# Block-sparse attention with a soft mixture of experts: wider value products for shared key blocks, and a new table of priorities

## The chip, the core and the metric

The kernel runs on one core of a Trainium2 chip. Its engines work side by side, each through its own list of instructions in the order of that list: TensorE (PE; its weight loads are shown apart as PEld), VectorE (DVE), ScalarE (ACT), GpSimd (POOL) and SyncE (SP), whose queue starts most DMA transfers. The metric is the device time of one execution in microseconds (us). Three runs of the kernel before took 310.15, 309.86 and 308.01 us; the median is 309.86.

## The reference

There are 4 batches of 8 heads, 768 positions and 64 dimensions. Positions are cut into 24 blocks of 32. A query block sees the key blocks beside it and itself, the first and the last block, and three sampled blocks; the first and the last query block see everything. What follows is a soft mixture of experts over all 3072 rows.

```python
mask = np.abs(blk_i - blk_j) <= 1
mask = mask | (blk_i == 0) | (blk_j == 0) | (blk_i == n_blocks - 1) | (blk_j == n_blocks - 1)
for qb in range(n_blocks):
    for kb in sampled_blocks[qb]:
        mask[qb * block:(qb + 1) * block, kb * block:(kb + 1) * block] = True
attn = softmax(where(mask, scale * q @ k.T, -1e9))      # softmax written out in the source
x = (attn @ v) as rows of 512                           # 8 heads side by side
logits = x @ phi                                        # 32 slots
slot_input = softmax(logits, axis=0).T @ x              # over all 3072 rows
slot_out = relu(slot_input @ w1[e]) @ w2[e]             # 8 experts, 4 slots each
out = softmax(logits, axis=1) @ slot_out
```

## The kernel before, in words

All data are fp32. One program matmul becomes two MATMUL instructions and two weight loads on the chip (a transpose on TensorE stays one of each).

**Attention.** The 22 inner query blocks of a batch are taken in pairs, called units. A first unit stands alone; the other ten form five tiles of two units, that is of four query blocks. For each query block `stage_k` (lines 450 to 478) copies the key blocks it sees into a staging tile `kst` of 256 columns, as eight places of 32: three neighbours, the first and the last block, three sampled ones. POOL copies the neighbours and first/last blocks, ACT or POOL the sampled ones. In the kernel before the neighbours stand at columns 0 to 95 or 32 to 127 by whether the block's number is odd or even, first and last at 128 to 191, and the sampled blocks in what is left. TensorE then makes the scores `s` (line 542), DVE the row maximum `nm` (557), ACT the exponential `p` (562), and DVE turns `p` by 32x32 blocks into `ptt` (569), so that place number c of the staging tile is row block c of `ptt`.

**Value products.** `av_heads` (642 to 675) multiplies the turned weights by the value blocks `v`, half of the heads at a time (`r` is 0 or 1; in each, `g` is the upper or lower 64 rows of TensorE). The weights are the stationary operand and the value block (130 columns: two heads of 64 and a column of ones) is moved past it. A half of a tile is, in this order: the first and last key block for all four query blocks (128 weight columns, 4 program matmuls); for each unit the two key blocks that both its query blocks see (64 columns, 8 matmuls); the one neighbour left to each query block (32 columns, 8 matmuls); and 24 sampled ones of 32 columns out of `vrs`, to which POOL copies the sampled value blocks (487). Each key block is thus multiplied unit by unit, although three query blocks in a row share it. There are 20 such tiles, so 40 halves, and 4 lone units. `av_mm` (line 634) issues every value product; the two query blocks that see everything (`dense`, 788 to 795) use it too, with 96 products in one go, called `avd`.

**After attention.** DVE divides by the sum of weights to give `x` (629); TensorE transposes it (`mxt`, 830), and four tiles form a group with logits `ml` (873), a transposed copy `lt` (891), transposed weights `md` (914), sums `ms` (923). At the end of attention a chain of small steps joins the groups, and the expert products (`pf`, `pso`) and output products (`po`) follow, with 33.6 MB of weights coming in by DMA and 6.3 MB of output leaving.

**Order.** Every step is a task with a cost, dependencies and a key: its number in the sequence plus an offset by its kind from the table `OFF` (lines 65 to 69). `Plan.run` (107 to 206) walks through them with its own costs and sets the order in which every engine gets its instructions. `ni`, the number of TensorE instructions of a task, enters there. So a new table gives another order on every engine.

Of the kernel before, what the change touches and what calls it, by code (L numbers as in the profile page):

```python
# [20 lines left out]
BLK, NB, NR = 32, 24, 3  # L21
# [9 lines left out]
VPOS = lambda k: (k - 1) % (NB + 1)  # L31
# [30 lines left out]
HEAD = -4096  # L62
SWITCH, FETCH, AHEAD, BLOCK = 0.22, 4.3, 0.5, 256
BACK = {"PE": 0.05, "DVE": -0.07, "ACT": -0.1, "POOL": -0.06, "SP": 0.0, "NONE": 0.0}
OFF = {"acc": 7.76, "av": -0.34, "av1": -0.31, "av2": -0.36, "avo": -1.17, "avo1": 1.4, "ce": -7.77, "cm": -0.63,
       "cn": 4.13, "dav": -0.96, "davo": -2.61, "dexp": 1.91, "do": 2.49, "dqk": -0.74, "dt": 2.51, "dtop": 9.1,
       "dtrn": -6.76, "exp": 1.01, "ldq": -0.52, "lexp": 1.53, "lg": -2.72, "lo": 1.64, "lp": -4.13, "lt": 3.97,
       "ltop": 3.66, "qk": -0.78, "scl": 15.38, "smp": 2.29, "sum": 2.97, "top": -2.96, "trn": -2.23, "vst": -2.29,
       "xt": 4.21, "xto": 3.13}
E_ = mybir.EngineType  # L70
MAN = {E_.PE, E_.DVE, E_.Activation, E_.Pool}
LAG = {"PE": 0.28, "DVE": 0.08, "ACT": 0.06, "POOL": 0.1, "SP": 0.0, "NONE": 0.0}
# [10 lines left out]
class Plan:  # L83
# [6 lines left out]
    def add(self, f, opts, deps, key, acq=(), byte=0, pre=None, pace=False, kind=None, mode=None, ni=0):  # L90
        t = Task(f, opts if isinstance(opts, list) else [opts], deps, key + OFF.get(kind, 0.0), acq, byte, pre, pace,
                 kind, mode, ni)
        self.tasks.append(t)
        return t
# [115 lines left out]
def attn_moe_kernel(ctx, tc, qT, kT, vfull, vtab, sampled, phi, w1, w2, out):  # L210
    nc = tc.nc
    PE, ACT, DVE, POOL, SP = nc.tensor, nc.scalar, nc.vector, nc.gpsimd, nc.sync
# [107 lines left out]
    ktile, vtile = [None] * B, [None] * B  # L320
# [6 lines left out]
    for n in range(NVR):  # L327
        n = (B * (NB - 2) + n) % NVR
        vrs[n] = pst.tile([P, 2, NR, 2 * D1], F32, name=f"vrs{n}")

    nq = [0]
# [54 lines left out]
    add = plan.add  # L386
# [17 lines left out]
    use = []  # L404
# [42 lines left out]

    fresh, nst, nvs = {}, [0], [0]

    def stage_k(b, i, n, use):  # L450
        k = nst[0] % NKST
        nst[0] += 1
        st, new = kst[k], fresh.get(k) != b
        fresh[k] = b

        w, r0 = (0, 96) if i % 2 else (32, 0)

        def fixed(t):
            kv = ktile[b]
            if new:  # L460
                POOL.tensor_copy(out=st[:, :, 128:192].rearrange("p c (g s) -> p c g s", g=2),
                                 in_=kv.rearrange("p c (g s) -> p c g s", g=NB)[:, :, 0:NB:NB - 1, :])
            POOL.tensor_copy(out=st[:, :, w:w + 96], in_=kv[:, :, (i - 1) * BLK:(i + 2) * BLK])  # L463

        def sampled_(t):
            for j, o in enumerate((r0, 192, 224)):
                src = ktile[b][:, :, ds(t.vals[j] * BLK, BLK)]
                if t.eng == "ACT":
                    ACT.activation(out=st[:, :, o:o + BLK], in_=src, func=AF.Copy, scale=1.0)  # L469
                else:  # L470
                    POOL.tensor_copy(out=st[:, :, o:o + BLK], in_=src)  # L471

        f = add(fixed, ("POOL", 0.95 if new else 0.52), [t_k[b]], n - 4, acq=[("kst", use)], kind="fix")
        r = add(sampled_, [("ACT", 0.72), ("POOL", 0.86)], [f, t_sreg], n - 2.5,
                pre=lambda e: block_numbers(sreg, i, e, NB - 1), kind="smp")
        k_use[b].extend([f, r])
        use.extend([f, r])
        return st, r
# [44 lines left out]
    def plan_pair(b, g, n):  # L523
        T = tile_of(b, (g + 1) // 2)
        w = 1 if g and g % 2 == 0 else 0
        u = Rec()
        u.g = g
        kd, ku = [], []
        for r in range(2):
            use = []  # L530
            kd.append(stage_k(b, 2 * g + 1 + r, n, use))
            ku.append(use)
        t_q, q_use = plan_q(u, b, g + 1, n)
        s_use = [[], []]
# [18 lines left out]
        for r in range(2):  # L553
# [21 lines left out]
            for j in range(2):  # L575
                t_e.append(add(lambda t, r=r, j=j, exp=exp: exp(t, r, j), ("ACT", 0.48), [t_m] + t_e, n + 0.2 + 0.01 * r, kind="exp",
                               acq=[("p", p_use)] if j == 0 else []))
            s_use[r].append(t_e[1])
            acq = []
            if w == 0:  # L580
                T.pt_use = getattr(T, "pt_use", {})
                T.pt_use[r] = []
                acq = [("ptt", T.pt_use[r])]
# [4 lines left out]
        for r in range(2):  # L588
            use = []
# [42 lines left out]
    def av_mm(av, o, m, g, r, lhsT, rhs, start, stop):  # L632
        av = av[g][o:o + m] if isinstance(av, list) else av[o:o + m, g]
        PE.matmul(av[:, r * 2 * D1:(r + 1) * 2 * D1].rearrange("p (a d) -> p a d", a=2),  # L634
                  lhsT=lhsT, rhs=rhs, start=start, stop=stop)

    G2 = [(g, slice(64 * g, 64 * g + 64)) for g in range(2)]

    def new_av(T):
        T.av = psA.tile([P, 2, 512], F32, tag="av", name="av", bufs=1)  # L640

    def av_heads(T, rs_):

        vt, us = vtile[T.b], T.units
        one = len(us) == 1
        m = 64 * len(us)
        for n, c in enumerate((4, 5)):
            for r in rs_:
                for g, s_ in G2:
                    av_mm(T.av, 64 * r if one else 0, m, g, r, T.pt[r][s_, c, 0:m // BLK].rearrange("p j q -> p (j q)"),  # L650
                          vt[s_, :, VPOS((0, NB - 1)[n]), r, :], n == 0, False)
        for c in (1, 2):
            for w, u in enumerate(us):
                for r in rs_:
                    for g, s_ in G2:
                        av_mm(T.av, 64 * r if one else 64 * w, 64, g, r,
                              T.pt[r][s_, c, 2 * w:2 * w + 2].rearrange("p j q -> p (j q)"),
                              vt[s_, :, VPOS(2 * u.g + c), r, :], False, False)
        for n in range(NR + 1):
            for w, u in enumerate(us):  # L660
                for r in rs_:
                    for j in range(2):
                        i = 2 * u.g + 1 + j
                        for g, s_ in G2:
                            if n == 0:

                                k, c = (i - 1, 0) if j == 0 else (i + 1, 3)
                                if k in (0, NB - 1):
                                    continue
                                v_ = vt[s_, :, VPOS(k), r, :]  # L670
                            else:
                                c = ((3, 0)[j], 6, 7)[n - 1]
                                v_ = u.vst[j][s_, :, n - 1, r, :]
                            av_mm(T.av, (64 * r if one else 64 * w) + 32 * j, 32, g, r, T.pt[r][s_, c, 2 * w + j], v_,
                                  False, n == NR)

    def plan_av(T, n):
        deps = T.turned + T.staged + [t_v[T.b]]
        use, x_use = [], T.x_use
        if len(T.units) == 1:  # L680
            def both(t):
                new_av(T)
                av_heads(T, range(2))

            def out(t):
                for r in range(2):
                    av_out(T, T.av, 64 * r, 64 * r + 64, slice(r, r + 1), 0)
            t_a = add(both, ("PE", 2.1), deps, n + 0.5, acq=[("av", use)], kind="av1", mode="63", ni=176)
            T.out = [add(out, ("DVE", 1.68), [t_a], n + 0.6, kind="avo1")]
        else:  # L690

            T.split = T is tiles.get((B - 1, NT - 1))

            def heads(t, r):
                if T.split and r == 0:
                    T.av = T.av0 = [psA.tile([P, 512], F32, tag="s", name="av", bufs=SB) for g in range(2)]
                elif r == 0 or T.split:
                    new_av(T)
                av_heads(T, (r,))
            if T.split:  # L700
                t_0 = add(lambda t: heads(t, 0), ("PE", 2.05), deps, n + 0.5, acq=[("s", use)] * 2, kind="av", mode="W3", ni=176)
                last = []
                t_a = add(lambda t: heads(t, 1), ("PE", 2.05), [t_0], n + 0.5, acq=[("av", last)], kind="av", mode="W3", ni=176)
                T.out = [add(lambda t, r=r: av_out(T, T.av if r else T.av0, 0, P, slice(r, r + 1)), ("DVE", 0.8 if r else 1.0),
                             [(t_0, t_a)[r]], n + 0.6, acq=[] if r else [("x", x_use)]) for r in range(2)]
                last.append(T.out[1])
            else:
                t_0 = add(lambda t: heads(t, 0), ("PE", 2.05), deps, n + 0.5, acq=[("av", use)], kind="av", mode="W3", ni=176)
                t_a = add(lambda t: heads(t, 1), ("PE", 2.05), [t_0], n + 0.5, kind="av2", mode="W3", ni=176)
                T.out = [add(lambda t: av_out(T, T.av, 0, P), ("DVE", 1.2), [t_a], n + 0.6, acq=[("x", x_use)], kind="avo")]  # L710
        x_use.extend(T.out)
        use.extend(T.out)
        v_use[T.b].append(t_a)
        T.t_av = t_a
        for u in T.use + list(T.pt_use.values()):
            u.append(t_a)
        if T.t:
            done.append((n, T))
# [346 lines left out]
    for gi in range(6):  # L1065
        Ts = done[4 * gi:4 * gi + 4]
        t_m, k = plan_group(gi, Ts, Ts[-1][0])
# [400 lines left out]
```

## Time and profile before

| | |
|---|---|
| median of 3 runs | 309.86 us |
| profiled execution | 306.71 us, its span 304.9 us, mean granted TensorE clock 0.976 |
| PE busy / in the chain that ended last | 90% / 77% |
| DVE, POOL, ACT busy | 72%, 60%, 54% |
| attention | from about 13 us to about 242 us of the span |

A busy share is a mean over stages. In the profile a MATMUL's time is counted from its start to a modelled end, and many overlap; what one costs is therefore read from the distance between starts, that is from the length of a stretch and the number of matmuls in it, not from its mean duration. "Issue" is idle time for which the profile shows no event that was waited for. The instruction queue of a page's part 3 (q8) is the DMA that brings TensorE's own instructions.

### The profile page before, as it was taken

To read this page: it belongs to the slowest core of one execution; us is meant where nothing else is said; L and a number is where in the kernel's file an instruction comes from. 1 tells how busy PE (TensorE), PEld (TensorE's weight loads), DVE (VectorE), ACT (ScalarE), POOL (GpSimd) and SP (SyncE) were. 2 spreads that over 40 slices of the span, in tenths; PEclk is the share of its full clock that TensorE was granted. 3 is DMA by queue.
4 is the path that set the end of the run, shared out by engine and by line. 5 is a ranking of instruction groups with operands and counts; after the bars stand their busy time and mean duration, and the time that the engine had idled before them with its cause. 6 is when DMAs were issued, how large, how long until landed. Compare 5 with 4: busy or idle time off the path is not lost.

```text
span 304.9 us, 17513 instructions
## 1 busy us (share of the span) xinstructions
PE 273.1 (90%) x7139; PEld 188.7 (62%) x7139; DVE 220.3 (72%) x497; ACT 165.2 (54%) x504; POOL 182.4 (60%) x509
## 2 busy tenths in 40 slices
PE   7599997998999999999989899969987989999950
PEld 7248675775867666777667666847655653355640
DVE  4699967869998689998979899958886545012360
ACT  0877866733966578286687646657633141102450
POOL 2579698696858999593889959329953314000000
PEclk9889999999999999999999999999999899999995
DMA  7936678440375751054666122878889997999998
GB/s 241 402 121 184 183 205 220 132 138 23 93 199 161 196 159 41 6 147 132 185 185 171 45 73 77 206 161 229 218 221 382 406 378 256 399 408 408 359 315 277
DMA packets 31633, 63.61 MB, mean 209 GB/s; under 512 B 5313, under 2 KB 18754, under 8 KB 31554
## 3 DMA queue, kind: packets, MB, share of 16 engines
q1 hardware_dynamic: 31408, 62.37, 64.5%
q8 instruction: 56, 0.92, 1.3%
q14 instruction: 23, 0.19, 0.2%
q10 hardware_dynamic: 146, 0.13, 0.1%
HBM read 56.19 MB, written 6.29 MB: 205 GB/s over the span
## 4 chain that ended last, share of the span: by engine, by line
PE 77%; DVE 6%; issue 5%; DMA 4%; ACT 2%; SPq 1%; POOL 1%; POOLq 1%; DVEq 0%; ACTq 0%
PE av L634 32%; PE s L542 13%; PE avd L634 7%; PE pf L1266 5%; PE pso L1274 4%; PE mxt L830 4%; PE sd L738 3%; DMA out_dram<-ob 2%; PE ml L873 2%; PE ms L923 2%; DMA ktile<-in_kT_dram 2%; DVE ptt L569 1%; DVE cm L1001 1%; PE po L1370 1%; PE pc L1029 1%
## 5 line engine op out<-in xcount | busy, mean ns | idle before, releaser
L487 POOL COPY vrs<-v 128x260 f32 x264 | 95.6, 412 | 24.1 <-PE av L634 16.1
L562 ACT ACTIVATE p<-s,nm 128x256 f32<-128x256 f32 x176 | 72.3, 479 | 23.7 <-DVE nm L557 21.7
L634 PE MATMUL av<-v,ptt 64*64 64x130 f32 (+2 forms) x1728 | 76.0, 288 | 1.6 <-issue 1.3
L634 PEld LDWEIGHTS av<-v,ptt 64*64 64x64 f32 (+2 forms) x1728 | 50.9, 133 | 29.6 <-issue 16.0
L569 DVE STREAM_TRANSPOSE ptt<-p 128x512 f32<-128x512 f32 x88 | 58.7, 692 | 10.1 <-ACT p L562 9.8
L542 PE MATMUL s<-kst,q 64*32 64x256 f32 x1408 | 51.3, 384 | 7.9 <-ACT pd L769 3.5
L557 DVE TENSOR_REDUCE nm<-s 128x2 f32<-128x512 f32 x88 | 55.0, 673 | 3.5 <-PE s L542 3.3
L463 POOL COPY kst<-ktile 128x384 f32<-128x384 f32 x88 | 42.7, 515 | 19.8 <-PE s L542 19.2
L634 PE MATMUL av<-vrs,ptt 64*32 64x130 f32 x2112 | 47.2, 276 | 3.2 <-issue 3.0
L469 ACT ACTIVATE kst<-ktile 128x128 f32 x171 | 38.7, 305 | 11.3 <-PE s L542 10.1
L542 PEld LDWEIGHTS s<-kst,q 64*32 64x32 f32 x1408 | 28.4, 106 | 21.5 <-issue 5.4
L634 PEld LDWEIGHTS av<-vrs,ptt 64*32 64x32 f32 x2112 | 36.2, 106 | 5.8 <-issue 5.3
L769 ACT ACTIVATE pd<-sd,nb 128x384 f32<-128x384 f32 x32 | 16.7, 577 | 18.6 <-DVE nb L764 18.0
L471 POOL COPY kst<-ktile 128x128 f32 x93 | 23.6, 306 | 0.0
L634 PE MATMUL avd<-v,ptd 64*64 64x130 f32 x768 | 22.9, 271 | 0.4 <-DVE x L629 0.3
L634 PEld LDWEIGHTS avd<-v,ptd 64*64 64x64 f32 x768 | 21.7, 132 | 2.1 <-PE s L542 1.6
L380 ACT COPY xT<-mxt 128x512 f32<-128x512 f32 (+1 forms) x22 | 12.1, 567 | 13.0 <-PE mxt L830 12.7
L756 DVE TENSOR_REDUCE nm<-sd 128x1 f32<-128x384 f32 x32 | 16.2, 545 | 2.8 <-PE sd L738 2.8
L629 DVE TENSOR_TENSOR x<-av,rs 128x512 f32<-128x512 f32 (+2 forms) x28 | 16.9, 605 | 1.0
L773 DVE STREAM_TRANSPOSE ptd<-pd 128x384 f32<-128x384 f32 x32 | 16.3, 552 | 1.8 <-ACT pd L769 1.7
L506 POOL TENSOR_SCALAR q<-q 128x256 f32<-128x256 f32 x25 | 10.3, 415 | 11.9 <-DMA q<-in_qT_dram 11.2
L830 PE MATMUL mxt<-ident,x 128*128 128x128 f32 x96 | 14.0, 282 | 3.7 <-issue 1.9
(123 smaller groups left out, 268.5 us busy)
## 6 DMA issues: line engine op xcount, KB each, us to landing
w<-in_w_dram SPq DMA_DIRECT2D x20, 512.0 KB, 8.1
v<-in_w_dram SPq DMA_DIRECT2D x12, 512.0 KB, 10.2
q<-in_qT_dram SPq DMA_DIRECT2D x47, 128.0 KB, 2.9
w<-in_w_dram SPq DMA_DIRECT2D x44, 128.0 KB, 3.3
out_dram<-ob SPq DMA_DIRECT2D x22, 256.0 KB, 3.4
ktile<-in_kT_dram SPq DMA_DIRECT2D x48, 96.0 KB, 2.9
v<-in_w_dram SPq DMA_DIRECT2D x24, 128.0 KB, 4.4
kw<-in_w_dram SPq DMA_DIRECT2D x6, 512.0 KB, 9.1
```

Source lines behind the costliest of these rows:

```text
L463: POOL.tensor_copy(out=st[:, :, w:w + 96], in_=kv[:, :, (i - 1) * BLK:(i + 2) * BLK])
L469: ACT.activation(out=st[:, :, o:o + BLK], in_=src, func=AF.Copy, scale=1.0)
L471: POOL.tensor_copy(out=st[:, :, o:o + BLK], in_=src)
L487: POOL.tensor_copy(out=st[:, :, j:j + 1, :], in_=vf[:, :, ds(t.vals[j], 1), :])
L542: PE.matmul(u.s[r][32 * p:32 * p + 32, j, :], lhsT=u.q[s_, p, j, :], rhs=kd[j][0][s_, p, :], start=True, stop=True)
L557: DVE.tensor_reduce(out=u.nm[r], in_=u.s[r], axis=AX.X, op=ALU.max, negate=True)
L562: ACT.activation(out=u.p[r][:, j, :], in_=u.s[r][:, j, :], func=AF.Exp, bias=u.nm[r][:, j:j + 1], scale=1.0)
L569: DVE.transpose(out=T.pt[r][:, :, 2 * w:2 * w + 2, :].rearrange("p k j q -> p j k q"), in_=u.p[r].rearrange("p j (k q) -> p j k q", k=8))
L629: DVE.tensor_tensor(out=x, in0=a[:, :, :, 0:D], in1=rs[lo:hi].unsqueeze(3).to_broadcast([hi - lo, 2, 2 * n, D]), op=ALU.mult)
L634: PE.matmul(av[:, r * 2 * D1:(r + 1) * 2 * D1].rearrange("p (a d) -> p a d", a=2), lhsT=lhsT, rhs=rhs, start=start, stop=stop)
L769: ACT.activation(out=u.p[r][k], in_=u.s[r][k], func=AF.Exp, bias=u.nb[r], scale=1.0)
L830: PE.transpose(T.px[:, c, :], T.x[:, c * P:(c + 1) * P], ident)
```

## The change

1. `av_heads` calls a new function for the neighbours. It walks through the key blocks that a whole tile sees. A block seen by three query blocks of the tile gets one product of 96 weight columns where these start at row 0 of the tile; where they start at row 32 it is split in one of 32 and one of 64 columns. Per half of a tile this is 2 program matmuls of 96, 6 of 64 and 6 of 32 columns, where there were 8 of 64 and 8 of 32. They come after those of 128 columns, the widest first.
2. So that place c means the same key block for all four query blocks, `stage_k` gets the place `a` (0 to 3) of the query block in its tile: its neighbours stand in places a to a+2, first and last in places 6 and 7, the sampled blocks in the places left free. The copies have the same number and sizes as before.
3. `ni` goes from 176 to 168, and all offsets in `OFF` are new.

```diff
-OFF = {"acc": 7.76, "av": -0.34, "av1": -0.31, "av2": -0.36, "avo": -1.17, "avo1": 1.4, "ce": -7.77, "cm": -0.63,
+OFF = {"acc": 4.35, "av": -0.84, "av1": -0.64, "av2": -1.46, "avo": -2.52, "avo1": 0.46, "ce": 0.57, "cm": -1.57,
...
+    def free_slots(a):
+
+        return [c for c in range(6) if not a <= c < a + 3]
...
-        w, r0 = (0, 96) if i % 2 else (32, 0)
...
-            POOL.tensor_copy(out=st[:, :, w:w + 96], in_=kv[:, :, (i - 1) * BLK:(i + 2) * BLK])
+            POOL.tensor_copy(out=st[:, :, a * BLK:(a + 3) * BLK], in_=kv[:, :, (i - 1) * BLK:(i + 2) * BLK])
...
-            for j, o in enumerate((r0, 192, 224)):
+            for j, o in enumerate(c * BLK for c in free_slots(a)):
...
+    def av_window(T, rs_, width):
+
+        vt, us = vtile[T.b], T.units
+        one, nq = len(us) == 1, 2 * len(us)
+        for c in range(nq + 2):
+            k, lo, hi = 2 * us[0].g + c, max(c - 2, 0), min(c + 1, nq)
+            if k in (0, NB - 1):
+                continue
+            for lo, hi in ((lo, lo + 1), (lo + 1, hi)) if lo and hi - lo == 3 else ((lo, hi),):
+                if hi - lo not in width:
+                    continue
+                for r in rs_:
+                    for g, s_ in G2:
+                        av_mm(T.av, (64 * r if one else 0) + BLK * lo, BLK * (hi - lo), g, r,
+                              T.pt[r][s_, c, lo:hi].rearrange("p j q -> p (j q)"), vt[s_, :, VPOS(k), r, :], False, False)
...
+        for w in (3, 2, 1):
+            av_window(T, rs_, (w,))
+        for n in range(NR):
...
-                t_0 = add(lambda t: heads(t, 0), ("PE", 2.05), deps, n + 0.5, acq=[("av", use)], kind="av", mode="W3", ni=176)
+                t_0 = add(lambda t: heads(t, 0), ("PE", 2.05), deps, n + 0.5, acq=[("av", use)], kind="av", mode="W3", ni=168)
```

How the order on TensorE changes is shown at two places. The first is the beginning of one half of a tile (`av`) in the second batch; the numbers behind a name are buffers, the size is weight columns by moved columns, and xN counts program matmuls. Before:

```order
L634 MATMUL av<-v_69,ptt 128x130 x4
L634 MATMUL av<-v_69,ptt 64x130 x8
L634 MATMUL av<-v_69,ptt 32x130 x8
L634 MATMUL av<-vrs_103,ptt 32x130 x2
L634 MATMUL av<-vrs_104,ptt 32x130 x2
```

With the change:

```order
L636 MATMUL av<-v_69,ptt 128x130 x4
L636 MATMUL av<-v_69,ptt 96x130 x2
L636 MATMUL av<-v_69,ptt 64x130 x6
L636 MATMUL av<-v_69,ptt 32x130 x6
L636 MATMUL av<-vrs_103,ptt 32x130 x2
```

Two of the 64-column and two of the 32-column products have gone, and two of 96 columns are new; the products from `vrs` are as they were.

The second place is TensorE around the dense product (`avd`) of the fourth batch, where steps of the group before (`ms`, `lt`, `mxt`) stand between scores (`s`). Before:

```order
L923 MATMUL ms<-x,d 32x512 x4
L542 MATMUL s<-kst_93,q_99 32x256 x8
L542 MATMUL s<-kst_94,q_99 32x256 x8
L891 MATMUL lt<-ident,lp 128x128
L542 MATMUL s<-kst_95,q_100 32x256 x8
L542 MATMUL s<-kst_96,q_100 32x256 x8
L634 MATMUL avd<-v_69,ptd 64x130 x96
L542 MATMUL s<-kst_93,q_97 32x256 x8
L542 MATMUL s<-kst_94,q_97 32x256 x8
L830 MATMUL mxt<-ident,x 128x128 x8
L634 MATMUL av<-v_69,ptt 128x130 x4
```

With the change:

```order
L927 MATMUL ms<-x,d 32x512 x4
L544 MATMUL s<-kst_93,q_99 32x256 x8
L544 MATMUL s<-kst_94,q_99 32x256 x8
L544 MATMUL s<-kst_95,q_100 32x256 x8
L544 MATMUL s<-kst_96,q_100 32x256 x8
L636 MATMUL avd<-v_69,ptd 64x130 x96
L834 MATMUL mxt<-ident,x 128x128 x8
L544 MATMUL s<-kst_93,q_97 32x256 x8
L544 MATMUL s<-kst_94,q_97 32x256 x8
L636 MATMUL av<-v_69,ptt 128x130 x4
```

`lt` no longer stands between the scores ahead of the dense product, and the transposes `mxt` from behind two score products to directly behind `avd`. Elsewhere the moves are of this kind: steps of a group and transposes pass one half of a tile or one score product; the sequence of tiles is the same.

## Rows read from the trace of the kernel before

**Rows 1.** The page: busy time by engine (part 1) and the chain (part 4).

```profile
PE 273.1 (90%) x7139; PEld 188.7 (62%) x7139; DVE 220.3 (72%) x497; ACT 165.2 (54%) x504; POOL 182.4 (60%) x509
...
PE 77%; DVE 6%; issue 5%; DMA 4%; ACT 2%; SPq 1%; POOL 1%; POOLq 1%; DVEq 0%; ACTq 0%
PE av L634 32%; PE s L542 13%; PE avd L634 7%; PE pf L1266 5%; PE pso L1274 4%; PE mxt L830 4%; PE sd L738 3%; DMA out_dram<-ob 2%; PE ml L873 2%; PE ms L923 2%; DMA ktile<-in_kT_dram 2%; DVE ptt L569 1%; DVE cm L1001 1%; PE po L1370 1%; PE pc L1029 1%
```

**Rows 2.** Window of one stage: length, busy us (instructions) of PE, PEld, DVE, ACT, POOL, clock.

```profile
85.00:135.00 50.00, 48.20 (x1493) 34.05 (x1483) 43.85 (x96) 33.38 (x106) 41.02 (x115) 1.00 0.46 129
```

**Rows 3.** The chain of waits in order of time: start, length, what.

```profile
79.96 5.53 PE avd L634 x192
...
96.38 1.02 PE mxt L830 x8
...
105.67 2.36 PE av L634 x88
```

**Rows 4.** Windows of one half, tile av, PE alone: length, busy (matmuls running).

```profile
105.59:106.24 0.65, 0.64 (x8) 1.00 0.68 196
106.24:106.84 0.60, 0.60 (x18) 1.00 0.80 212
106.84:107.95 1.10, 1.10 (x68) 1.00 0.80 230
```

**Rows 5.** The same view, the first 128-column products one by one.

```profile
105.59:105.81 0.22, 0.21 (x2) 1.00 0.71 223
105.81:105.92 0.11, 0.11 (x4) 1.00 0.89 266
105.92:106.03 0.11, 0.11 (x6) 1.00 0.55 186
```

**Rows 6.** Groups by form on PE: count, busy us, mean ns, idle before.

```profile
L634 PE MATMUL av<-v,ptt 64*128 64x130 f32 x320 | 29.2, 300 | 0.2
```

**Rows 7.** Timeline of PE: start, length, line, shapes, count, idle time before.

```profile
90.28 0.31 PE L634 MATMUL av<-vrs,ptt 64*32 64x130 f32 x4 [0.58 <-issue]
90.40 0.37 PE L542 MATMUL s<-kst,q 64*32 64x256 f32 x1
90.42 0.28 PE L634 MATMUL av<-vrs,ptt 64*32 64x130 f32 x3
90.53 1.09 PE L542 MATMUL s<-kst,q 64*32 64x256 f32 x31
91.55 1.71 PE L634 MATMUL av<-v,ptt 64*128 64x130 f32 x40
93.05 0.95 PE L634 MATMUL av<-vrs,ptt 64*32 64x130 f32 x48
94.30 2.08 PE L542 MATMUL s<-kst,q 64*32 64x256 f32 x64 [0.29 <-issue]
```

**Rows 8.** The page, part 3: the queue that brings TensorE's instructions.

```profile
q8 instruction: 56, 0.92, 1.3%
```

**Rows 9.** Waits of PE: total us, times, longest us.

```profile
PE av L634 <- issue: 4.3, 6, 1.3
...
PE s L542 <- issue: 2.7, 3, 2.3
PE mxt L830 <- issue: 1.9, 1, 1.9
...
PE s L542 <- POOL vrs L487: 1.7, 1, 1.7
PE mxt L830 <- DVE x L629: 1.5, 2, 0.8
```

**Rows 10.** Timeline of PE: the three longest idle times marked issue.

```profile
74.46 0.78 PE L634 MATMUL av<-v,ptt 64*64 64x130 f32 x7 [1.30 <-issue]
...
201.75 1.08 PE L542 MATMUL s<-kst,q 64*32 64x256 f32 x28 [2.28 <-issue]
...
233.96 0.77 PE L830 MATMUL mxt<-ident,x 128*128 128x128 f32 x5 [1.91 <-issue]
```

More of the change, by code (lines that the diff above doesn't have):

```diff
@@ L64 @@
 BACK = {"PE": 0.05, "DVE": -0.07, "ACT": -0.1, "POOL": -0.06, "SP": 0.0, "NONE": 0.0}
-OFF = {"acc": 7.76, "av": -0.34, "av1": -0.31, "av2": -0.36, "avo": -1.17, "avo1": 1.4, "ce": -7.77, "cm": -0.63,
[L66 to L69, printed above, removed]
+OFF = {"acc": 4.35, "av": -0.84, "av1": -0.64, "av2": -1.46, "avo": -2.52, "avo1": 0.46, "ce": 0.57, "cm": -1.57,
+       "cn": 3.06, "dav": 0.22, "davo": 0.82, "dexp": -0.08, "do": 4.06, "dqk": -1.85, "dt": 2.26, "dtop": -0.71,
+       "dtrn": -6.45, "exp": 0.1, "ldq": 6.51, "lexp": 2.4, "lg": 0.27, "lo": 1.31, "lp": -0.77, "lt": 4.58, "ltop":
+       3.52, "qk": -0.87, "scl": 6.6, "smp": 1.49, "sum": 3.39, "top": -0.71, "trn": -2.36, "vst": -2.22, "xt": 3.08,
+       "xto": 3.1}
 E_ = mybir.EngineType
@@ L448, in attn_moe_kernel, with stage_k @@
     fresh, nst, nvs = {}, [0], [0]
-    def stage_k(b, i, n, use):
+    def free_slots(a):
+        return [c for c in range(6) if not a <= c < a + 3]
+    def stage_k(b, i, a, n, use):
         k = nst[0] % NKST
@@ L460, in fixed @@
             if new:
-                POOL.tensor_copy(out=st[:, :, 128:192].rearrange("p c (g s) -> p c g s", g=2),
+                POOL.tensor_copy(out=st[:, :, 192:256].rearrange("p c (g s) -> p c g s", g=2),
                                  in_=kv.rearrange("p c (g s) -> p c g s", g=NB)[:, :, 0:NB:NB - 1, :])
-            POOL.tensor_copy(out=st[:, :, w:w + 96], in_=kv[:, :, (i - 1) * BLK:(i + 2) * BLK])
+            POOL.tensor_copy(out=st[:, :, a * BLK:(a + 3) * BLK], in_=kv[:, :, (i - 1) * BLK:(i + 2) * BLK])
         def sampled_(t):
-            for j, o in enumerate((r0, 192, 224)):
+            for j, o in enumerate(c * BLK for c in free_slots(a)):
                 src = ktile[b][:, :, ds(t.vals[j] * BLK, BLK)]
@@ L530, in plan_pair @@
             use = []
-            kd.append(stage_k(b, 2 * g + 1 + r, n, use))
+            kd.append(stage_k(b, 2 * g + 1 + r, 2 * w + r, n, use))
             ku.append(use)
@@ L646, in av_heads @@
         m = 64 * len(us)
-        for n, c in enumerate((4, 5)):
+        for n, c in enumerate((6, 7)):
             for r in rs_:
@@ L651, in av_heads @@
                           vt[s_, :, VPOS((0, NB - 1)[n]), r, :], n == 0, False)
[L652 to L659, printed above, removed]
+        for w in (3, 2, 1):
+            av_window(T, rs_, (w,))
+        for n in range(NR):
             for w, u in enumerate(us):
@@ L662, in av_heads @@
                     for j in range(2):
-                        i = 2 * u.g + 1 + j
+                        a = 2 * w + j
                         for g, s_ in G2:
[L665 to L675, printed above, removed]
+                            av_mm(T.av, (64 * r if one else 0) + BLK * a, 32, g, r, T.pt[r][s_, free_slots(a)[n], a],
+                                  u.vst[j][s_, :, n, r, :], False, n == NR - 1)
     def plan_av(T, n):
@@ L700, in plan_av @@
             if T.split:
-                t_0 = add(lambda t: heads(t, 0), ("PE", 2.05), deps, n + 0.5, acq=[("s", use)] * 2, kind="av", mode="W3", ni=176)
+                t_0 = add(lambda t: heads(t, 0), ("PE", 2.05), deps, n + 0.5, acq=[("s", use)] * 2, kind="av", mode="W3", ni=168)
                 last = []
-                t_a = add(lambda t: heads(t, 1), ("PE", 2.05), [t_0], n + 0.5, acq=[("av", last)], kind="av", mode="W3", ni=176)
+                t_a = add(lambda t: heads(t, 1), ("PE", 2.05), [t_0], n + 0.5, acq=[("av", last)], kind="av", mode="W3", ni=168)
                 T.out = [add(lambda t, r=r: av_out(T, T.av if r else T.av0, 0, P, slice(r, r + 1)), ("DVE", 0.8 if r else 1.0),
@@ L707, in plan_av @@
             else:
-                t_0 = add(lambda t: heads(t, 0), ("PE", 2.05), deps, n + 0.5, acq=[("av", use)], kind="av", mode="W3", ni=176)
-                t_a = add(lambda t: heads(t, 1), ("PE", 2.05), [t_0], n + 0.5, kind="av2", mode="W3", ni=176)
+                t_0 = add(lambda t: heads(t, 0), ("PE", 2.05), deps, n + 0.5, acq=[("av", use)], kind="av", mode="W3", ni=168)
+                t_a = add(lambda t: heads(t, 1), ("PE", 2.05), [t_0], n + 0.5, kind="av2", mode="W3", ni=168)
                 T.out = [add(lambda t: av_out(T, T.av, 0, P), ("DVE", 1.2), [t_a], n + 0.6, acq=[("x", x_use)], kind="avo")]
```

## The prediction, made before the changed kernel ran

> **What bounds the kernel now.** I read the page first. TensorE is busy 90% of the span and holds 77% of the chain that ended last, 32% in the value products of one line and 7% in the dense ones [rows 1]. The reader is to see that whatever a value product costs on TensorE stands in the time nearly in full, while POOL and ACT, which copy the keys, are not in the chain. In the stage from 85 to 135 us TensorE is busy 48.2 of 50.0 us at the full granted clock of 1.00 (2.4 GHz), and DVE 43.9 us [rows 2]: DVE is the next one behind it.
>
> Then I took one half of a tile apart. In the chain it lasts 2.36 us [rows 3]. Windows show three stretches: 0.65 us for 8 MATMULs of 128 weight columns, 0.60 us for 16 of 64, 1.10 us for 64 of 32 [rows 4]; of the counts there, 2 and 4 still run on from the stretch before. Inside the first stretch two MATMULs start in each 0.11 us: the number running grows 2, 4, 6, while each runs for some 0.30 us [rows 5, 6]. The dense product, of 64 columns, has 192 MATMULs in 5.53 us, which is four in each 0.115 us [rows 3]. With eight at a time of 32 columns, 64 take eight steps, 0.88 of the 1.10 us. So all three widths go in **rounds of about 0.11 us**, with two, four or eight matmuls side by side: 4 + 4 + 8 = 16 rounds, 1.76 us, and the rest of the 2.36 us (0.60) is the passage between widths. What counts is rounds, not matmuls.
>
> The second thing to see is a limit beside the array. PE's idle time marked issue is 4.3 + 2.7 + 1.9 = 8.9 us in ten waits, three of them long (1.30, 2.28 and 1.91 us, 5.5 together), seven short (3.4 together) [rows 9, 10]. Between the waits that end at 90.28 and at 94.30 us stand 4+1+3+31+40+48 = 127 matmuls [rows 7], with their weight loads 254 instructions. TensorE has 2 x 7139 = 14,278 instructions [rows 1] and its instruction queue has 56 packets [rows 8]: 255 instructions to a packet. I read these short waits as TensorE having used up one packet of instructions before the next is there; this one then came 4.02 us after the last.
>
> **The change, part by part.**
>
> *Rounds.* The two program matmuls of 96 columns are four MATMULs. 96 columns fit neither the four-fold nor the eight-fold side-by-side, so I cost them like those of 128: two at a time, two more rounds, 0.22 us in each half. What is taken away shortens nothing: of the 12 MATMULs of 64 columns left, eight still go to the upper 64 rows of the result, and two side by side make four rounds, as now; of the 32-column ones, three of the four places still have eight in each half of the array, so eight rounds stay. 40 halves x 0.22 = **+8.8 us**, all on TensorE and so in the chain. No row shows a width of 96. Bounds: if the narrower stretches shrink with their number of matmuls (0.44 x 4/16 = 0.11 and 0.88 x 4/64 = 0.06 us), 0.05 a half, +2 us; if each pair costs its share of the whole first stretch (0.65/4 = 0.16, so 0.32 a half), +13 us. I stay with the round, the nearest row.
>
> *Fewer instructions.* A half has 168 where it had 176, 320 less in all, 1.25 packets. A packet with one half in it now holds 3.73 us of work (4.02 less the wait of 0.29 [rows 7]); with 0.22 us for the new rounds and eight instructions more until its end (8 x 2.36/176 = 0.11) it holds 4.06 us. That is the 4.02 us after which the next packet was there, so the short waits close: 3.4 us, and about 0.15 us more for each of the seven, because idle time is counted only from the modelled end of a matmul of 0.30 us where the next would have started 0.11 us on and its end 0.15 us before: 4.5 us. In the three long ones the packet itself seems late or something else is waited for; they shrink by what a packet of one and a half halves gains, 0.5 us each: 1.5 us. Together **-6.0 us**; bounds 0 (the waits have another cause) and -10.4 (8.9 + 10 x 0.15, all gone).
>
> Here a rule speaks against the change. The row shows waits 254 instructions apart, on an engine that was not waiting for data [rows 7]. The Trainium skill, "Runtime: NRT & Kernel Launch", section "Instruction fetch mechanics", says that an engine's instructions come in blocks of 256 while it works on the one before, and that this is mostly hidden behind issue. By it the waits would not be of this kind, and saving instructions would save nothing; that is the first rival below. The rows agree with the size of the block and not with the hiding.
>
> *Waits for other engines.* TensorE waits 1.7 us for POOL, early, and up to 0.8 us for DVE's `x` before a transpose [rows 9]. POOL and DVE get no more work; TensorE reaches the first place after four halves (0.9 us later), the second after two (0.5 us): **-1.4 us**, bounds 0 and -2.5.
>
> *Staged keys.* Copies are as many and as large; only columns change. Nothing, on engines outside the chain; if POOL or ACT were late, it would show as more of the waits just named.
>
> *The order.* Where the transposes `mxt` now pass two score products, those scores come 1.02 us later [rows 3], and with them DVE's maxima, ACT's exponentials and the next half, whose products of the tile before cover 2.4 us; `lt`, `ms` and `md` are short. Nothing is removed by this. I set 0, bounds -3 and +3: about two waits of 1.7 us, taken away or made new.
>
> Sum: 8.8 - 6.0 - 1.4 = **+1.4 us**. The profiled execution took 306.7 us, so 308.1; that execution lies 3.2 us under the median of the runs, 309.9, so **311.3 us** as a median. The bounds of its terms give about 307 to 315 when not all fall on one side.
>
> **Rivals.**
>
> 1. *The waits are not for instructions* (slower). The array gets 8.8 us more, none of the issue waits closes, the waits for POOL and DVE shrink: +7.4, 317.3 us. It decides from the point where PE's issue idle stays above some 6 us. For it: the three longest waits, 5.5 of 8.9 us, fit no regular refill. Against it: the distance of the short ones [rows 7]. 0.20.
> 2. *The new order takes away the long waits as well* (faster): what is left of the three, 4.0 us, and of the waits for POOL and DVE, 1.1 us, goes: 1.4 - 5.1 = -3.7, 306.2 us. For it: two of them stand at a score product and at the transposes, where steps were moved [rows 10]. Against: the sequence of tiles is the same, and no wait is taken away by name. 0.22.
> 3. *The change does not cost rounds* (faster): the 96-column products lie under the passage between widths, 0.60 us a half, and the saving of 1.25 packets of 4.02 us is kept where TensorE waits for them: -5 us, 305 us. 0.07.
> 4. *The new order makes new waits* (slower): 1.4 + 3 = +4.4, 314.3 us. DVE, 88% busy in the stage [rows 2], has least room for scores that come late. 0.08.
>
> My forecast keeps 0.43.
>
> **How the numbers follow.** 1% is 3.1 us, about what a measurement of this kernel tells from no change. Faster: rivals 2 and 3, 0.29, less 0.01 for what of rival 2 ends within 1%: 0.28. Slower: rivals 1 and 4, 0.28, and 0.01 of the forecast's upper end: 0.29. The rest, 0.43, is within 1%. The range reaches down to rival 3 and up to rival 1: 304.5 to 317.5 us; the forecast's own is 308 to 314, since the order can't be read from the trace.
>
> **What would show it.** In the profile after: the widest MATMULs of `av` (128 and 96 columns) go from 320 to 480, those of 64 columns from 768 to 608 and all MATMULs from 7139 to 6979; a half without waits lasts 2.58 us in the chain instead of 2.36; PE's idle marked issue falls from 8.9 to about 4 us. If a half stays at 2.36 us, the first term is wrong; if it is 2.58 and issue stays, the second; if both hold and the time still differs by over 1%, it is the order, and new or missing long waits of PE at `s`, `av` or `mxt` would say where. The forecast would be wrong altogether if the granted clock fell below 1.00 in the stage.

## The result, and the profile after

The changed kernel took 304.04 us (median of 18 runs, 302.25 to 311.57), the kernel before on the same chip 310.06 (18 runs, 305.25 to 317.55). The ratio is **0.9876, 95% interval 0.9836 to 0.9917**: faster by 1.2%, some 3.8 us. I had forecast 311.3 us, within 1% of before, and 304.5 us as the lower end of the range. The ratios here leave out runs that were disturbed by a lower clock, medians and ranges are over all runs, and four of the profiles below (the old table's first, all split, more instructions, second half) are of such longer runs.

The page of the changed kernel: busy time by engine, and the chain.

```profile
PE 278.9 (92%) x6979; PEld 196.9 (65%) x6979; DVE 216.3 (72%) x498; ACT 165.8 (55%) x505; POOL 181.5 (60%) x507
...
PE 76%; DVE 9%; issue 4%; POOL 3%; POOLq 2%; ACT 2%; ACTq 0%; DVEq 0%
PE av L636 32%; PE s L544 11%; PE avd L636 6%; PE pso L1278 5%; PE pf L1270 5%; PE sd L742 3%; PE mxt L834 3%; PE ml L877 3%; POOLq L368 2%; PE po L1374 2%; PE st L402 2%; PE ms L927 2%; DVE x L631 1%; DVE nm L760 1%; DVE ptd L777 1%
```

Against [rows 1], TensorE has more to do, 278.9 us instead of 273.1, in a span that is 2.9 us shorter (302.0). So by the page what went is idle time. The window from 85 to 135 us, which answers to [rows 2], says it in one row (length, busy us of PE, PEld, DVE, ACT, POOL, clock): 50.00 us of 50.00, where it was 48.20.

```profile
85.00:135.00 50.00, 50.00 (x1484) 37.76 (x1470) 43.78 (x96) 33.71 (x108) 42.83 (x122) 1.00 0.43 123
```

The cost of the wide products is as forecast. In the chain (start, length, what) halves of a tile last 2.58 us, against 2.36 in [rows 3]:

```profile
86.52 2.57 PE av L636 x80
...
90.00 2.59 PE av L636 x79
...
111.18 2.58 PE av L636 x81
```

Windows of one half, tile `av` alone, answer to [rows 4, 5]. The four stretches are the products of 128, 96, 64 and 32 columns:

```profile
111.11:111.66 0.55, 0.55 (x8) 0.55 (x10) 0.00 (x0) 1.00 0.23 73
111.66:111.98 0.32, 0.32 (x8) 0.17 (x4) 0.00 (x0) 1.00 0.69 231
111.98:112.58 0.60, 0.60 (x14) 0.43 (x12) 0.00 (x0) 1.00 0.26 77
112.58:113.69 1.11, 1.11 (x62) 0.90 (x60) 0.00 (x0) 1.00 0.28 92
```

The 96-column products go two in each 0.11 us, as those of 128 do. The 64-column stretch still takes 0.60 us, with 12 MATMULs instead of 16, and the last 1.11 instead of 1.10 us with 60 instead of 64: fewer matmuls, the same rounds. The groups by form have the counts that the change gives, 320 + 160 wide, 608 of 64 columns (one was [rows 6]):

```profile
L636 PE MATMUL av<-v,ptt 64*64 64x130 f32 x608 | 32.1, 284 | 0.1
L636 PE MATMUL av<-v,ptt 64*128 64x130 f32 x320 | 28.7, 296 | 1.1 <-DVE x L631 1.0
...
L636 PE MATMUL av<-v,ptt 64*96 64x130 f32 x160 | 15.5, 269 | 0.0
```

Now the waits of PE from the first dense product to the last value product (total, times, longest), against [rows 9]:

```profile
PE av L636 <- issue: 1.5, 1, 1.5
PE av L636 <- DVE x L631: 1.0, 1, 1.0
PE s L544 <- POOL kst L473: 0.4, 1, 0.4
PE avd L636 <- DVE x L631: 0.3, 1, 0.3
PE mxt L834 <- DVE x L631: 0.3, 1, 0.3
PE s L544 <- POOL kst L463: 0.3, 1, 0.3
PE s L544 <- issue: 0.2, 1, 0.2
```

Issue is 1.7 us where it was 8.9. Of the three long waits [rows 10] those of 1.30 and 2.28 us are gone and one of 1.5 us is left, in the last tile; of the short ones [rows 7] one of 0.2 us is left. The wait for POOL fell from 1.7 to 0.7. New is 1.0 us for DVE's `x` before `av`. The queue of TensorE's instructions has one packet less than in [rows 8]:

```profile
q8 instruction: 55, 0.90, 1.3%
```

Two windows of that same stretch, the kernel before first, hold the balance: its length, and PE's busy time.

```profile
23.04:241.50 218.46, 205.86 (x6325) 151.21 (x6326) 185.85 (x397) 135.58 (x427) 164.65 (x464) 0.99 0.57 162
```

```profile
22.86:237.19 214.33, 210.27 (x6166) 158.34 (x6166) 181.28 (x397) 136.75 (x429) 164.73 (x464) 1.00 0.56 160
```

The stretch is 4.1 us shorter: idle time went from 12.6 to 4.1 us (-8.5), busy time rose by 4.4, half of what forty halves at +0.22 us make. What follows gives 1.4 us back. A spell at half clock of the same 3.4 us lies inside the stretch in the kernel before, and just behind it in the changed one, so it favours the changed kernel in the stretch alone, by at most 1.7 us (before first):

```profile
235.50:238.90 3.40, 3.40 (x66) 2.74 (x69) 2.35 (x12) 0.00 (x0) 1.74 (x4) 0.50 1.03 410
```

```profile
238.70:242.10 3.40, 3.24 (x36) 2.53 (x35) 0.43 (x2) 0.37 (x1) 0.99 (x2) 0.50 1.03 417
```

### The profile page after: what moved, and what is told of

Read it like the earlier page. It is cut to its first block, busy times and chain, and to the rows that moved or that the text cites. A ratio compares the mean times of both kernels' runs of the same rounds, so it can differ in the third digit from the quotient of the medians.

```text
span 302.0 us, 17240 instructions
## 1 busy us (share of the span) xinstructions
PE 278.9 (92%) x6979; PEld 196.9 (65%) x6979; DVE 216.3 (72%) x498; ACT 165.8 (55%) x505; POOL 181.5 (60%) x507
## 4 chain that ended last, share of the span: by engine, by line
PE 76%; DVE 9%; issue 4%; POOL 3%; POOLq 2%; ACT 2%; ACTq 0%; DVEq 0%
PE av L636 32%; PE s L544 11%; PE avd L636 6%; PE pso L1278 5%; PE pf L1270 5%; PE sd L742 3%; PE mxt L834 3%; PE ml L877 3%; POOLq L368 2%; PE po L1374 2%; PE st L402 2%; PE ms L927 2%; DVE x L631 1%; DVE nm L760 1%; DVE ptd L777 1%
## 5 line engine op out<-in xcount | busy, mean ns | idle before, releaser
L636 PE MATMUL av<-v,ptt 64*64 64x130 f32 (+3 forms) x1568 | 83.0, 285 | 1.1 <-DVE x L631 1.0
L636 PEld LDWEIGHTS av<-v,ptt 64*64 64x64 f32 (+3 forms) x1568 | 57.5, 136 | 29.4 <-issue 13.9
L544 PE MATMUL s<-kst,q 64*32 64x256 f32 x1408 | 49.8, 384 | 4.4 <-ACT pd L773 3.5
L636 PE MATMUL av<-vrs,ptt 64*32 64x130 f32 x2112 | 50.3, 276 | 1.5 <-issue 1.5
L465 POOL COPY kst<-ktile 128x384 f32<-128x384 f32 x88 | 42.5, 510 | 15.2 <-PE s L544 12.6
L471 ACT ACTIVATE kst<-ktile 128x128 f32 x168 | 38.0, 306 | 5.8 <-PE s L544 4.1
L636 PEld LDWEIGHTS av<-vrs,ptt 64*32 64x32 f32 x2112 | 37.5, 105 | 2.3 <-issue 2.3
L473 POOL COPY kst<-ktile 128x128 f32 x96 | 24.3, 299 | 0.0
L380 ACT COPY xT<-mxt 128x512 f32<-128x512 f32 (+1 forms) x21 | 11.4, 569 | 15.4 <-PE mxt L834 14.9
L742 PE MATMUL sd<-ktile,q 64*32 64x384 f32 x256 | 17.7, 509 | 0.4 <-ACT p L564 0.4
L629 DVE TENSOR_SCALAR rs<-av 128x8 f32<-128x8 f32 (+2 forms) x28 | 4.3, 155 | 18.4 <-PE av L636 18.2
```

Source lines behind the costliest of these rows:

```text
L465: POOL.tensor_copy(out=st[:, :, a * BLK:(a + 3) * BLK], in_=kv[:, :, (i - 1) * BLK:(i + 2) * BLK])
L544: PE.matmul(u.s[r][32 * p:32 * p + 32, j, :], lhsT=u.q[s_, p, j, :], rhs=kd[j][0][s_, p, :], start=True, stop=True)
L742: PE.matmul(u.s[r][k][32 * p:32 * p + 32, :], lhsT=T.dq.q[s_, p, j, :], rhs=kt[s_, p, 384 * k:384 * (k + 1)], start=True, stop=True)
```

## The experiments

Two theories stood at first. F, later called P (the same one): TensorE's instructions come in packets of 256, about 4.0 us apart (4.02 in [rows 7]); fewer instructions, and more work in each packet, let TensorE stop waiting for them. O: the new table of priorities did it. Unless said otherwise, each kernel is the changed one but for its diff. The first four ran beside each other, then three, then three.

**The table alone, both ways.** The wide products with the old table:

```diff
-OFF = {"acc": 4.35, "av": -0.84, ...    # the table of the change
+OFF = {"acc": 7.76, "av": -0.34, ...    # the table of before
```

> The changed kernel with the old table of offsets: products of 96 columns and the new staging, the old priorities. Theory F (instruction packets: the wider products give each packet of 256 instructions more work, so TensorE no longer runs out of them): a half of a tile 2.58 us, PE idle marked issue at most 3 us, time within 1% of the changed kernel, 301 to 307 us. Theory O (the new order took the waits away, the products only cost): issue idle stays at 7 to 9 us and the time is 8 to 9 us over the changed kernel, 311 us or more.

308.57 us (304.97 to 314.2); before on that chip 311.68. Ratio 0.9954, interval 0.9899 to 1.001. Issue idle is 2.9 us, as F has it, but the median lies above F's 301 to 307 us, and under the 311 of O. And the kernel before with the new table:

```diff
-OFF = {"acc": 7.76, "av": -0.34, ...    # in the kernel before
+OFF = {"acc": 4.35, "av": -0.84, ...
```

> The kernel before with the new table of offsets alone: old products (16 rounds a half), old staging. Theory F: a half 2.36 us, issue idle 6 us or more as before, time within 1% of the kernel before. Theory O: issue idle about 2 us as in the changed kernel and, without the 8.8 us of the wide products, 294 to 299 us.

310.62 us (307.45 to 321.43), ratio 1.0043 (0.9987 to 1.0099); issue idle 5.5 us, a little under the 6 of F and far from the 2 of O. The new table without the wide products gains nothing: theory O falls. What it adds to them stayed open here, and was run again below.

**New order, narrow products.** Each 96-column product split into 64 and 32 columns, everything else as in the change:

```diff
-... if lo and hi - lo == 3 else ((lo, hi),):
+... if lo and hi - lo == 3 else ((0, 2), (2, 3)) if hi - lo == 3 else ((lo, hi),):
```

> The changed kernel, each product of 96 columns made as one of 64 and one of 32; sequence of steps on every engine, staging and table as in the changed kernel. So rounds and instruction count of a half are those of before (16 and 176), in the new order. Theory F: a half 2.36 us, issue idle 6 to 10 us, time 2 to 8 us over the changed kernel. Theory O: issue idle about 2 us and 8 to 9 us under the changed kernel, 293 to 297 us.

308.12 us, ratio 0.9978 (0.9916 to 1.0039). The gain is gone as far as the interval tells, and the issue waits are back, 7.9 us in the stretch, with the order of the change untouched. The largest:

```profile
PE av L636 <- issue: 3.5, 8, 0.8
PE mxt L834 <- issue: 2.3, 1, 2.3
PE ml L877 <- issue: 1.0, 2, 0.5
```

**Wide in the first half of each tile only** (the same split where `r` is 1):

```diff
+... else ((0, 2), (2, 3)) if hi - lo == 3 and rs_[0] else ((lo, hi),):
```

> As the run with all 96-column products split, but only for the second half of each tile (20 of 40 halves); order as in the changed kernel. Theory F: array time 4.4 us less than in the changed kernel, issue idle 3 to 6 us against 1.7, so the time about that of the changed kernel, within 1%. Theory O: 4 to 5 us under the changed kernel, issue idle unchanged.

305.13 us (301.73 to 307.37), ratio 0.9876 (0.9789 to 0.9963): half of the wide products gives the whole gain. Issue idle in the stretch is 1.8 us, less than the 3 to 6 that I expected.

**More instructions, hardly any work.**

```diff
+        if not one:
+            for n in range(3):
+                for g, s_ in G2:
+                    av = T.av[g] if isinstance(T.av, list) else T.av[:, g]
+                    PE.matmul(av[32 * n:32 * n + 32, 400 + rs_[0]:401 + rs_[0]], lhsT=T.pt[rs_[0]][s_, 6, n],
+                              rhs=vt[s_, 0, VPOS(0), rs_[0], 0:1], start=True, stop=True)
```

> The changed kernel with six program matmuls more at the end of each half of a tile: 32 weight columns, one moved column, into columns of the result that nobody reads. Order and table stay; a half has 192 TensorE instructions instead of 168. Theory P (packets of 256 instructions, about 4.0 us apart at the least): a tile of two halves and four score products has 2 x 192 + 4 x 64 = 640 instructions, 2.50 packets, 10.0 us at 4.0 us each, against 2 x 2.58 + 4 x 1.06 = 9.4 us of work and what the new products take themselves (0.05 to 0.1 us a half); some 0.5 us are missing in a tile. PE's issue idle goes from 1.7 back to 6 to 10 us, in waits about 256 instructions apart, and the time is 311 to 317 us. Theory O (the new order took the waits away): issue idle stays under 3 us, and the time grows by the products' own 2 to 4 us only, to 306 to 308 us.

318.7 us (309.87 to 319.99); before on that chip 315.96 (305.22 to 321.01). One run took 309.87 us, at a mean granted clock of 0.986; the other five took 315.52 to 319.99, at 0.949 to 0.973. So the median, above what I expected, says little; the one run is just under the 311 to 317 of P and above the 306 to 308 of O. The theories differ more in the waits. The execution with the profile took 318.34 us, but its granted clock was 1.00 throughout the stretch of attention. That stretch, its waits of PE, and the queue's packets:

```profile
23.27:247.28 224.01, 216.26 (x6645) 167.09 (x6646) 179.77 (x397) 137.05 (x429) 164.22 (x463) 1.00 0.54 154
```

```profile
PE av L636 <- issue: 4.3, 7, 1.1
...
PE avd L636 <- issue: 0.8, 2, 0.6
PE s L544 <- issue: 0.5, 1, 0.5
PE av L684 <- issue: 0.4, 1, 0.4
...
PE ml L883 <- issue: 0.3, 1, 0.3
```

```profile
q8 instruction: 59, 0.97, 1.4%
```

Issue idle is 6.3 us there, in an order that has 1.7 without these products. The stretch is 224.0 us instead of 214.3. The shortest halves, from their start to the start of what follows, lasted 2.46 instead of 2.39 us, so I put the new products' own work at 40 x 0.07 = 2.8 us; the other 6.9 are the price of their 960 instructions in this execution. The run of 309.87 us speaks for a smaller price, but it has no profile.

**No 96-column products at all** (the output lacks them):

```diff
-        for w in (3, 2, 1):
+        for w in (2, 1):
```

> The changed kernel without its two products of 96 columns in each half (the output lacks them); order and table stay. It prices them. If the two cost two rounds of 0.11 us, as predicted, a half lasts 2.36 us instead of 2.58. Theory P: a tile has 576 instructions, 2.25 packets, 9.0 us, against 8.96 us of work, so hardly any packet is late: issue idle 1 to 3 us, and nearly all of the 8.8 us come off: 295 to 298 us. Rival D (DVE is next): with a half of 2.36 us TensorE waits for DVE's x or ptt instead, and the time is 299 to 302 us. Rival W (the wide products cost no rounds): a half stays near 2.55 us and the time at 303 to 304 us.

300.53 us (298.76 to 306.1), ratio 0.9786 (0.9703 to 0.987). A half is back at 2.36 us, so Rival W falls:

```profile
105.10 2.36 PE av L636 x77
```

The rounds can be priced by the busy time of tile `av` on PE in the same stretch. Changed kernel, then this one, then the kernel before:

```profile
22.86:237.19 214.33, 113.73 (x3592) 1.00 0.56 160
```

```profile
24.41:233.91 209.50, 104.47 (x3431) 1.00 0.57 159
```

```profile
23.04:241.50 218.46, 108.82 (x3751) 0.99 0.57 162
```

The wide products cost 113.73 - 104.47 = 9.3 us. The third row tells what I had missed. The kernel before has the same 16 rounds a half as this one, but 176 instructions instead of 160, and is busy 4.4 us longer. At most 1.7 of that is clock, in the window from 235.5 to 238.9 us shown above. The other 2.7 us are halves stretched by packets that came late by less than the modelled end of the matmul still running: lost time that shows as busy. The trace of the kernel before has it: eleven of its halves last 2.58 to 2.73 us at full clock instead of 2.36, 3.3 us together, and in each the MATMUL that starts late lies, to within three, a whole multiple of 128 MATMULs from a wait marked issue (or ends such a wait itself). Without the wide products two halves are so stretched, by 0.7 us together. The time came out above my 295 to 298 us, because other waits took the place, as Rival D has it, POOL's even more than DVE's:

```profile
PE s L544 <- POOL kst L463: 1.7, 1, 1.7
PE av L636 <- DVE x L631: 1.6, 2, 0.9
...
PE s L544 <- POOL q L508: 0.4, 1, 0.4
PE s L544 <- POOL vrs L489: 0.4, 1, 0.4
```

**Wide in the second half only** (the mirror: `not rs_[0]` in the diff above).

> The changed kernel with the 96-column products split into 64 and 32 columns in the first half of every tile, so that only the second half has wide ones (the mirror of the run in which only the first half has them). Theory P: 600 instructions in a tile, 2.34 packets, 9.4 us, against 9.2 us of work: 0.2 us missing in a tile, of which dense products and transposes give some back; issue idle 2 to 4 us, time 302 to 306 us, as with the wide products in the first half alone. Theory O: the time is that of the split run plus half of nothing, 307 to 309 us, as the order is the same as in the run with all products split.

306.97 us (301.55 to 309.0), ratio 0.9856 (0.9766 to 0.9946): the same as the first half only within what these runs can tell, so it counts how many are wide, not which. Issue idle is 4.4 us, somewhat above the 2 to 4 expected; 2.0 of it is one wait in the last tile.

**Three side by side, once more.** The changed kernel, the old table with wide products, and the first half wide, with the diffs above:

> The changed kernel as it is, beside the next two on the same chip, to settle what the new table adds once the products are wide. In the one profile of each, the stretch from the first dense product to the last value product was 214.3 us here and 216.1 us with the old table, of which 3.4 us at half clock (1.7 us lost) in the latter: without that both are the same. Theory P (only instructions and rounds count): 303 to 305 us, and the old table within 1% of it.

> The changed kernel with the table of before, all products wide. Theory P: within 1% of the changed kernel on this chip, ratio to before about 0.987. Theory O2 (the new table is worth its own 0.8% once the products are wide, as the first comparison with its wide interval gave): 2 to 4 us slower than the changed kernel, ratio about 0.995.

> The changed kernel with wide products in the first half of each tile alone. Theory P: a tile has 600 instructions, 2.34 packets, 9.4 us at 4.0 us each, against 9.2 us of work; with all wide it has 592 instructions, 9.25 us, against 9.4 us of work. Both end at about 9.4 us a tile, so the time is the same as the changed kernel's within 1%. Should the dense products and transposes give the packets their 0.2 us a tile back, it is up to 4 us faster: in its one profile the stretch from the first dense product to the last value product was 212.2 us against 214.3 us.

Changed 307.41 us (303.6 to 310.36), old table 307.91 (306.34 to 312.96), first half wide 304.21 (301.75 to 305.45), six runs each; before on that chip 315.81 (306.29 to 320.74). The changed kernel's median lies above the 303 to 305 that I expected. The ratios between the three are worked out from means and spread, with runs left out as above. Old table 308.0 (five runs) against changed 306.7 (five): 1.004, 95% interval 0.996 to 1.012. With wide products the table of before does as well within what this can tell, though the first comparison, 0.9954 against 0.9876, allows the new one some 0.8%. Half wide 303.9 (six) against the changed 306.7: 0.991, interval 0.983 to 0.998. In the first comparison the two had one ratio, 0.9876. Whether the version with half of the wide products is better by up to 1%, or the same, stays open; it is not worse. No ratio to the kernel before comes from this chip; two of its eleven runs would be left for it.

**The grid.** One count needs no new kernel. If a wait marked issue is a wait for a packet, then between two such waits lies a whole multiple of 128 MATMULs, each with its weight load. Counted in the traces from one issue wait to the next (some records are missing, and other instructions of TensorE are not counted, so a little less is to be expected):

```
kernel                 MATMULs between issue waits, over 128
before                 3.99 3.88 0.99 1.98 1.98 1.98 8.88 9.88 0.99 1.99 0.98 1.00 1.98
narrow, new order      0.98 2.98 1.95 3.97 0.98 0.99 1.00 0.98 1.00 5.90 4.95 1.98 8.87 1.99 0.98 1.00 1.98
more instructions      2.98 1.00 1.98 9.88 1.98 5.91 0.99 6.91 12.86 1.98 0.99
```

All fall on the grid as far as that lets one tell, the short distances to within 0.05. So do, in the other runs, the short distances between waits of 0.15 us or more. In the kernel before, the three longest [rows 10] are at 3.99, 9.88 and 1.98, and so were waits for a packet like the short ones.

## Why the prediction was wrong

*Rounds, +8.8.* Right: 2.58 us a half, two 96-column MATMULs in each 0.11 us, 9.3 us from the run without them.

*Fewer instructions, -6.0.* **This is the step that failed, in its size.** The mechanism held: adding instructions brought the waits back, and so did splitting the wide products. (The kernel's own planner had it in its source: `on_pe` reckons with BLOCK = 256 instructions, and with FETCH = 4.3 us for each.) But I wrote that in the three long waits "the packet itself seems late or something else is waited for", and let each shrink by 0.5 us; they lie on the grid too, and two went altogether. And I added 0.15 us a wait for what idle time doesn't show. Measured: 7.7 us less issue idle in the stretch (9.4 to 1.8, the smallest waits counted in), and about 2.7 us of stretched halves. That is 10.4 us, which was the far end of my own bounds.

The balance by tile says why half of the wide products is enough. A tile is two halves and two score steps of 32 MATMULs, 1.9 us for both, as the chain of the kernel before has them:

```profile
112.20 1.89 PE s L542 x64
```

Some of my expectations counted four score steps, which adds 2.0 us to the packets of a tile and some 2.3 to its work; the table has two:

```
                     instructions   x 4.0/256   work of halves and scores   issue idle in the stretch
narrow (before)          480          7.5 us          6.6 us                     9.4 us
half of them wide        472          7.4             6.8                        1.8
all wide                 464          7.25            7.05                       1.8
no 96 columns            448          7.0             6.6                        1.3
more instructions        512          8.0             7.1                        6.3
```

In every row the packets need longer than the work. Where they need up to some 0.5 us longer, little issue idle is left (4.4 us in the mirror of the second row, 2.0 of it one wait at the end); where it is 0.9, it is large. So longer steps between the tiles, such as the transposes (16 instructions in 1.02 us), seem to give back about half a microsecond a tile. That is a reading of these five rows, and 4.0 us is not a constant (see the end). It also shows what my sum had wrong beside the size: as long as TensorE waits for packets, added rounds fill time that it would have waited, and what counts is the packets saved. The change saves 320 instructions, 1.25 packets, 5.0 us at 4.0 each, and the stretch became 4.1 us shorter. Without the wide products, 320 instructions fewer again, it is 4.8 us shorter still. Half wide does not fit: it has 160 instructions more than all wide, and its stretch is 2.1 us shorter (212.2). There the work already counts.

*The rule of the Trainium skill* ("Runtime: NRT & Kernel Launch", "Instruction fetch mechanics": blocks of 256, mostly hidden behind issue) led to rival 1, 317.3 us. The grid agrees with the size of the block. It is not hidden here: 9.4 us of issue idle in the stretch before, each wait at a block's end.

*Waits for other engines, -1.4.* All idle time but issue fell by 0.9 us: POOL's 1.7 to 0.7, but 1.0 us new, for `x` before `av`, behind the two scores that now follow `mxt`. That is the place that I named under the order: rival 4 in small.

*Order, 0 within 3 us; staged keys, 0.* Borne out: the table alone 1.0043; with wide products 1.004 between the tables in one comparison, up to 0.8% the other way in the other. The copies made no wait beyond the 0.7 us for POOL.

The sum as measured, in the stretch: rounds +9.3, packets -10.4, other waits -0.9, clock at most -1.7 (the changed kernel has its spell at half clock just behind the stretch), other tiles' busy time -0.5: in all -4.1 us, but for rounding. It closes by construction, as these terms are differences of the same windows; what was measured apart are the 2.58 us of a half and the eleven stretched halves. Against my sum, +1.4, the span came out 2.9 us shorter. The other 3.0 us of the miss are the step from the profiled execution to the median: I added 3.2 us, from three runs before, and with the change the two lie 0.2 us apart (303.82 and 304.04). Rival 2 had the right size, -3.7, and the right waits, but the wrong cause: it let the order take them away. Rival 3, 305 us, had the nearest time and the right price of the saved packets, -5 us, but took the rounds to be free, and a half did not stay at 2.36 us. Both were near by luck.

## What to carry to other kernels

Where TensorE's idle time is marked issue, count the MATMULs between two such waits. If they are multiples of 128, as here, where each MATMUL has a weight load of its own, long waits and short ones have the same cause, and the kernel has a second bound, packets times their distance, beside the array: compare both for one tile. While packets are the later ones, fewer and wider matmuls may even cost array time and still gain; once the waits are gone, going further gains nothing, as all wide against half wide shows. And lost time is not only idle time: compare the busy time of the same work between two kernels.

## What the runs showed of the hardware

A wait can cost more than its own time. In the run with the old table, the second time, windows of PE around a wait of 1.93 us for instructions in the last tile, and behind it (PE busy first, then PEld, DVE, ACT, POOL, the clock, DMA share, GB/s):

```profile
232.00:236.50 4.50, 4.15 (x101) 3.32 (x104) 3.52 (x15) 0.20 (x1) 3.77 (x10) 1.00 1.01 401
236.50:239.80 3.30, 1.44 (x53) 1.10 (x53) 0.10 (x1) 0.00 (x0) 0.00 (x0) 1.00 1.02 403
239.80:246.60 6.80, 5.95 (x56) 3.75 (x55) 2.04 (x7) 1.66 (x6) 0.98 (x2) 0.50 1.03 404
```

PE was busy 1.44 of 3.30 us, and then for 6.8 us the granted clock was 0.50, that is 1.2 instead of 2.4 GHz, while it was busy 5.95 us: up to 3 us lost. The same stands behind the wait of 1.91 us at 233.96 in the kernel before [rows 10] and, for 3.4 us, behind that of 1.51 us in the changed one. It is not peculiar to packets: in the same run with the old table TensorE waited 1.56 us for POOL, was busy 1.94 us of the 3.50 from 48.6 to 52.1, and then had a clock of 0.50 for 3.4 us. And it does not follow every wait: behind that of 2.28 us at 201.75 [rows 10] the clock stayed at 1.00.

Packets came later where DMA was busier. In all traces together, between 20 and 255 us, there are 24 places where two issue waits (of 0.1 us or more) lie one packet apart; the distance from end to end of the two waits is the distance of the packets. At a DMA share of 0.36 to 0.74 it was 3.73 to 5.02 us (12 places), at 0.78 to 0.94 it was 4.28 to 5.47 (6), at 1.01 to 1.03 it was 6.06 to 7.11 (6). The last six all lie at the end of attention, behind 228 us, so something else at that end is not ruled out. Of the long waits those of 1.91, 1.93 and 1.51 us lie where the share is 0.99 or above, and so does that of 2.28 us; the one of 1.30 us does not (0.16). That the traffic is what makes a packet late is likely by these numbers but not shown: no run took it away.
